# Loads of the first attention group in 112 + 16 rows, two more products of ones, and a new order of the opening pieces

## The chip, the cores and the metric

The kernel runs on one core of a Trainium2 chip. The metric is the device time of one execution in microseconds (us), lower is better. The profile is one further execution, taken by the hardware profiler. Its span runs from the first to the last instruction. TensorE (PE) does matrix products, VectorE (DVE) and ScalarE (ACT) work on elements, GpSimd (POOL) does a little set-up and issues some transfers, and SyncE (SP) only issues transfers.

## The reference

A normalised linear attention feeds a two-layer block with a gate. B = 8 batches, 8 heads, S = 576 positions, head width 64; the block has 4608 tokens, width 512 and hidden width 2048. All arrays come in as float64 or float32 and are multiplied in float32 or in two float32r parts.

```python
kv  = einsum('bhsd,bhse->bhde', k, v)
out = einsum('bhsd,bhde->bhse', q, kv)
x   = out / sqrt(mean(out*out, -1) + 1e-6) * g_norm     # then heads side by side: (B*S, 512)
h   = x @ w_in                                          # 512 -> 2048
g   = h * erf(softplus(h))
y   = g @ w_out                                         # 2048 -> 512
```

## The kernel before

**Groups.** The 4608 rows are taken as nine groups of 512: T = 0 to 7 are the first 512 positions of each batch, and T = 8 is made of the last 64 positions of all batches. A group needs its attention output transposed, `xT` (four slices, one for each pair of heads p = 0 to 3), before its first layer can start. The first two groups (T = 0 and 1, `FIRST = 2`) multiply plain float32; the later ones use weights cut into three float32r parts, written to DRAM and loaded back by SyncE.

**The opening, T = 0.** `load_pair` (L137) loads k, v and q of a pair of heads. `first_group(p)` (L712) defines thirteen small steps for a pair: `kv` (L717, products of k and v on TensorE), `kv_out` (L731, VectorE copies them to SBUF), `q` (L736, TensorE transposes q), `q_out` (L742, ScalarE copies), `result` (L746, TensorE), `square` (L749, ScalarE), `mean` (L752, TensorE), `log`, `root`, `again` (L756 to L763, ScalarE) and `norm_a`, `norm_b`, `norm_c` (L766 to L776, VectorE; the last writes slice p of `xT`). `tail`, `tail_out`, `tail_result` and `tail_kept` (L793 to L817) do the last 64 positions of batch 0. In what order all these steps are put into the programs of the engines is written out by hand in the string `ORDER`. No scheduler changes it: each engine takes its own instructions in the order in which the Python code issues them.

**The weights.** They come as float64 and are turned into float32 in 18 items (`w_order`, L301): w_in columns 0 to 3 one by one, then pairs of w_in or w_out tiles. An item is loaded (`load_w`, four raw buffers), split (`w_split`, L266) and joined (`w_join`, L277). `w_next(what)` (L308) takes the next item of that kind, with a counter of its own for load, split and join. A split of the opening gives ScalarE two instructions, e (L273) and m (L274). After the opening, `w_late` is set (L849) and a split gives it m alone; then the join begins with e on VectorE (L284). A join is L287, L290 and L297 on VectorE, and L297 reads e and m:

```python
    def weights():
        w_next("split")
        w_next("join")
        w_next("load")
```

`ORDER` holds five `split`, four `join` (each with a load) and four `fetch` (four of the waiting transfers of later batches each).

**The loop.** `for n in range(FIRST * FC + 1)` takes one 128-wide slice of the hidden layer at a time: products with w_in (L970), the copy out of PSUM (L983) and softplus (L1001) on ScalarE, erf after every fourth n (L915), the gate product `gates(n - 4)` on VectorE (L911), and `project(n - 5)` on TensorE (L673), which reads the gated slice and w_out. At n = 0 ten blocks are issued at once, of n = 0 to 2: `(0,0) (1,0) (0,1) (1,1) (2,0) (2,1) (0,2) (1,2) (2,2) (0,3)`, where (n, c) needs item n of w_in and slice c of `xT`; then come (1,3) at n = 1, (2,3) at n = 2, and four blocks for each n from 3 on. Whether `weights()` runs at an n, once before and once after the attention pieces of that n, is decided by `due` (L904) from the count of joins alone: items 4 to 9 are joined at n = 2, 4, 5, 6, 7, 8, items 10 and 11 at n = 9, 12 at 10, 13 at 11, items 14 and 15 at n = 12, 16 at 13 and 17 at 14. After the `weights()` of an n come the pieces of the next group's attention (`norm` and `turn`, then later `visit` with L432 to L446 on TensorE), and `gates` behind them.

**The start.** Two products of a 128x512 tile of ones (L828) run on TensorE while the first loads are under way.

Of the kernel before, what the change touches and what calls it, by code (L numbers as in the profile page):

```python
# [39 lines left out]
FP32 = mybir.dt.float32  # L40
# [17 lines left out]
SHIFT = 4096.0  # L58
SQ = 32
ORDER = """  # L60
kv0 q0 q_out0 kv_out0 result0 kv1 q1 square0 mean0 kv_out1 q_out1 log0 result1
kv2 kv_out2 root0 square1 q2 again0 q_out2 mean1 norm_a0 tail norm_b0 log1 tail_out
kv3 q3 root1 again1 q_out3 split norm_c0 kv_out3 tail_result result2 result3 square2 split mean2
next0 fetch square3 norm_a1 split mean3 log2 root2 norm_b1 tail_kept again2
join fetch log3 root3 join next1 again3 softplus norm_c1 join fetch norm_a2 split norm_b2 norm_c2 norm_a3
norm_b3 norm_c3 split join fetch
"""


# [1 line left out]
def kernel(  # L71
# [10 lines left out]
    nc = tc.nc  # L82
    P = 128
    B, H, S, D = q.shape
    DM, DF = moe_w_in.shape[0], moe_w_in.shape[1] // 2
    J = 4
    G = J * P
    R = S - G
    NP = H // 2
# [35 lines left out]

    q_last = early.tile([P, 2, 2, D], FP32, name="q_last", bufs=1)

    def chunks(T):

        return 6 if T == 0 else 5  # L130

    def rows_in(T, c):

        rows = S // chunks(T) // 16 * 16
        return rows + (S - chunks(T) * rows if c == 0 else 0)

    def load_pair(i, later=False):  # L137
        T, p = divmod(i, NP)
        if T >= B:
            return  # L140
        pool = early if i in (2, 3) else kvp
        for name, got, src in (("k", k_sb, k), ("v", v_sb, v)):
            side = nc.scalar if (i, name) == (0, "v") else nc.sync
            C = chunks(T)
            rows, rest = rows_in(T, 1), rows_in(T, 0) - rows_in(T, 1)
            t = got[T, p] = pool.tile([rows + rest, 2, C, D], FP32, name=f"{name}_sb", tag=name)
            heads = src[T, 2 * p : 2 * p + 2]
            due_ = [
                partial(
                    side.dma_start,  # L150
                    out=t[:rows].rearrange("r h c d -> r h (c d)"),
                    in_=heads[:, : S - rest].rearrange("h (r c) d -> r h (c d)", c=C),
                )
            ]
            if rest:
                due_.append(
                    partial(
                        side.dma_start,
                        out=t[rows:, :, 0],
                        in_=heads[:, S - rest :].rearrange("h r d -> r h d"),  # L160
                    )
                )
            if later:
                to_fetch.extend(due_)
            else:
                for start in due_:
                    start()
        if T > 0:
            load_q(i)
            return  # L170
        t = pool.tile([P, G if pool is early else S], FP32, name="q_sb", tag="q")
        t = q_sb[T, p] = t[:, 0:G].rearrange("p (j h d) -> p j h d", j=J, h=2)
        nc.sync.dma_start(
            out=t, in_=q[T, 2 * p : 2 * p + 2, 0:G, :].rearrange("h (p j) d -> p j h d", j=J)
        )
# [35 lines left out]
    ones = early.tile([P, G], I32, name="ones", tag="w_m", bufs=2).bitcast(FP32)  # L211
# [10 lines left out]
    bd_first = early.tile([P, 2, P], FP32, name="bd_first", bufs=1)  # L222
    nc.vector.memset(bd_first, 0.0)
    nc.gpsimd.memset(bd_kv, 0.0)
    for p in range(NP):
        nc.gpsimd.dma_start(
            out=q_last[p % 2 * R : p % 2 * R + R, p // 2],
            in_=q[0, 2 * p : 2 * p + 2, G:S, :].rearrange("h r d -> r h d"),
        )
    for i in range(2):  # L230
        nc.gpsimd.dma_start(
            out=g_col[i * D : i * D + D, :], in_=g_norm.rearrange("(d one) -> d one", one=1)
        )
# [120 lines left out]
    def kv_products(T, p, at, crossed):  # L354


        ks, vs = (x.pop((T, p)) for x in (k_sb, v_sb))
        C = chunks(T)
        for c in range(C):
            for r in range(2):  # L360
                rows = (slice(0, D), slice(D, rows_in(T, c)))[r]
                for i in range(2):
                    yield partial(
                        nc.tensor.matmul,
                        at[rows_of[i], 1 - (r ^ i) if crossed else r, kv_cols],
                        lhsT=ks[rows, i, c],
                        rhs=vs[rows, i, c],
                        start=(c == 0),
                        stop=(c == C - 1),
                    )  # L370

    def kv_kept(T, p, at):
# [339 lines left out]
    def first_group(p):  # L712

        st = {}
        bd = bd_first[:, p] if p < 2 else kv_of(0, p)

        def kv():  # L717
            st["kv"] = ps_at.tile([P, G], FP32, name="kv_ps", tag="at")
            ks, vs = (x.pop((0, p)) for x in (k_sb, v_sb))
            C = chunks(0)  # L720
            for c in range(C):
                for i, s in enumerate(rows_of):
                    nc.tensor.matmul(  # L723
                        st["kv"][s, s],
                        lhsT=ks[0 : S // C, i, c],
                        rhs=vs[0 : S // C, i, c],
                        start=(c == 0),
                        stop=(c == C - 1),
                    )

        def kv_out():  # L731
            kv_ps = st.pop("kv")
            for s in rows_of:
                nc.vector.tensor_copy(out=bd[s, s], in_=kv_ps[s, s])

        def q():  # L736
            o = st["o"] = ps_o.tile([P, G], FP32, name="o_ps", tag=f"o{p}")
            qs = q_sb.pop((0, p))
            for j in range(J):
                nc.tensor.transpose(o[:, j * P : j * P + P], qs[:, j], ident)  # L740

        def q_out():  # L742
            st["u"] = gate.tile([P, G], FP32, name="qT", tag="h")
            nc.scalar.copy(st["u"], st["o"])

        def result():  # L746
            nc.tensor.matmul(st["o"], lhsT=bd, rhs=st["u"], start=True, stop=True)  # L747

        def square():  # L749
            nc.scalar.activation(st["u"], st["o"], AF.Square)  # L750

        def mean():  # L752
            ms = st["ms"] = ps_h.tile([P, G], FP32, name="ms_ps", tag="h")
            nc.tensor.matmul(ms, lhsT=mean_w.bitcast(FP32), rhs=st["u"], start=True, stop=True)  # L754

        def log():  # L756
            st["r"] = gate.tile([P, G], FP32, name="rms_r", tag="s")
            nc.scalar.activation(st["r"], st["ms"], AF.Ln, bias=eps_col)

        def root():  # L760
            nc.scalar.activation(st["r"], st["r"], AF.Exp, scale=-0.5)

        def again():  # L763
            nc.scalar.activation(st["u"], st["r"], AF.Square)

        def norm_a():  # L766
            nc.vector.scalar_tensor_tensor(
                out=st["u"], in0=st.pop("ms"), scalar=EPS, in1=st["u"], op0=ALU.add, op1=ALU.mult
            )

        def norm_b():
            nc.vector.scalar_tensor_tensor(
                out=st["u"], in0=st["u"], scalar=3.0, in1=st.pop("r"), op0=ALU.subtract, op1=ALU.mult
            )

        def norm_c():  # L776
            if p == 0:
                xT[0] = wide.tile([P, KC, G], FP32, name="xT", tag="a")
            nc.vector.scalar_tensor_tensor(
                out=xT[0][:, p, :],  # L780
                in0=st.pop("o"),
                scalar=gm_col,
                in1=st.pop("u"),
                op0=ALU.mult,
                op1=ALU.mult,
            )

        steps = (kv, kv_out, q, q_out, result, square, mean, log, root, again, norm_a, norm_b, norm_c)
        return {step.__name__ + str(p): step for step in steps}

# [31 lines left out]
    def join_load():  # L822
        w_next("join")
        w_next("load")

    warm = ps_h.tile([P, G], FP32, name="warm_ps", tag="h")
    for _ in range(2):
        nc.tensor.matmul(warm, lhsT=ones[:, 0:P], rhs=ones, start=True, stop=True)  # L828
    for _ in range(RAW):
        w_next("load")  # L830
    do = {
# [1 line left out]
        "tail_out": tail_out,  # L833
        "tail_result": tail_result,
        "tail_kept": tail_kept,
        "split": partial(w_next, "split"),
        "softplus": softplus_table,
        "join": join_load,
# [78 lines left out]
    for n in range(FIRST * FC + 1):  # L917
        T, f = divmod(n, FC)
# [38 lines left out]
        elif T < FIRST:  # L957
# [11 lines left out]
            for i, c in blocks:  # L969
                nc.tensor.matmul(  # L970
                    plain[i],
                    lhsT=w_in_sb[:, i % FC, c],
                    rhs=xT[T][:, c, :],
                    start=(c == 0),
                    stop=(c == KC - 1),
                )
        if T < FIRST:
            if n == whole:
                old_h = acc.tile([P, BATCH, G], FP32, name="h", tag="e")
            h = hs[n] = old_h[:, n - whole] if n >= whole else unit("h_sb")  # L980
# [92 lines left out]
    for m in range(first_batch, batches + 1):  # L1073
        T, b = divmod(m, NB)
        todo = []
        last_ = b == NB - 1 and T + 1 < NG
        if T + 1 < NG:
            todo = list(attention(T + 1, b, in_parts=last_))
            if b == 0:
                side = late_r if T % 2 == FIRST % 2 else late  # L1080
# [135 lines left out]
```

## Time and profile before

| what | us |
|---|---|
| median of three timed runs | 907.28 (906.86 to 907.31) |
| the profiled execution's own time | 908.57 |
| its span | 906.8 |
| TensorE busy | 897.8 |
| VectorE busy | 749.3 |
| ScalarE busy | 593.4 |
| GpSimd busy | 4.7 |
| TensorE busy in 0 to 24 us | 20.52 |
| TensorE busy in 24 to 142 us | 117.75 |
| TensorE busy in 142 to 880 us | 737.14 |
| TensorE busy in 880 to 907 us | 22.38 |

A line of the timeline gives the start in us, the duration in us, the engine, the line of the code, the instruction, what it writes and reads, the tile's size and the number of instructions merged, and in square brackets how long the engine had been idle and what ended that. A line of windows gives for each stretch its length, then the busy time of PE, PE's weight loads, DVE, ACT and POOL with the number of instructions, then the granted TensorE clock as a share of full speed, the busy share of the DMA engines and GB/s. A float32 product shows as two MATMUL records.

### The profile page before, as it was taken

How to read it: one execution, taken by the hardware profiler on the slowest of the kernel's cores; microseconds unless marked ns; L12 is line 12 of the kernel's file. 1: busy time of each engine (PE TensorE's matmuls, PEld its weight loads, DVE VectorE, ACT ScalarE, POOL GpSimd, SP SyncE). 2: the span in 40 equal slices, each digit the busy share in tenths (PEclk: the TensorE clock that was granted, in tenths of full speed). 3: DMA queues.
4: the chain of work that ended last, by engine and by line, in shares of the span. 5: the costliest groups of instructions: out<-in, count | busy, mean ns of one | idle time of the engine just before them, and what ended most of it. 6: DMA issues, size and time to landing. Idle time of an engine off the chain costs nothing.

```text
span 906.8 us, 13592 instructions
## 1 busy us (share of the span) xinstructions
PE 897.8 (99%) x4994; PEld 667.9 (74%) x4994; DVE 749.3 (83%) x1085; ACT 593.4 (65%) x784; POOL 4.7 (1%) x14
## 2 busy tenths in 40 slices
PE   8999999999999999999999999999999999999998
PEld 4444446666678888888888888888888888888886
DVE  4899958997688888888888888888888888887777
ACT  5976667775766666666666666666666666665552
POOL 2000000000000000000000000000000000000000
PEclk9999999999999999999999999999999999999999
DMA  9978408999699999999899989999897788778871
GB/s 275 296 213 238 113 16 292 357 357 348 204 342 338 331 325 297 354 324 311 282 315 340 319 280 313 349 328 307 270 352 271 266 315 306 288 282 323 313 265 49
DMA packets 145506, 259.91 MB, mean 287 GB/s; under 512 B 81504, under 2 KB 104032, under 8 KB 145440
## 3 DMA queue, kind: packets, MB, share of 16 engines
q1 hardware_dynamic: 144640, 258.09, 84.7%
q10 hardware_dynamic: 608, 0.82, 0.3%
q8 instruction: 40, 0.66, 0.3%
q14 instruction: 26, 0.21, 0.1%
q0 software_dynamic: 192, 0.13, 0.1%
HBM read 224.40 MB, written 34.60 MB: 286 GB/s over the span
## 4 chain that ended last, share of the span: by engine, by line
PE 94%; ACT 2%; DMA 2%; DVE 1%; issue 0%; SPq 0%; DVEq 0%; ACTq 0%
PE n_ps L617 48%; PE m_ps L617 24%; PE o_ps L673 10%; PE h_ps L970 6%; PE at_ps L446 2%; PE at_ps L432 2%; DMA w_out_parts<-w_out 1%; PE at_ps L484 1%; PE at_ps L485 1%; DMA q_sb<-in_q_dram 1%; PE ms_ps L754 0%; PE o_ps L747 0%; PE kv_ps L723 0%; PE o_ps L740 0%; DVE h L911 0%
## 5 line engine op out<-in xcount | busy, mean ns | idle before, releaser
L617 PE MATMUL n_ps<-w_out_parts,g_forms 128*128 128x512 f32 x928 | 230.5, 390 | 0.6 <-DMA w_out_parts<-w_out 0.6
L617 PE MATMUL n_ps<-x_forms,w_in_parts 128*128 128x512 f32 x896 | 224.3, 392 | 0.0
L617 PEld LDWEIGHTS n_ps<-w_out_parts,g_forms 128*128 128x128 f32 x928 | 172.7, 188 | 36.5 <-DMA w_out_parts<-w_out 1.1
L617 PEld LDWEIGHTS n_ps<-x_forms,w_in_parts 128*128 128x128 f32 x896 | 166.6, 188 | 35.7 <-issue 0.2
L595 DVE TENSOR_TENSOR h<-m_ps,h 128x512 f32<-128x512 f32 x116 | 78.1, 687 | 69.0 <-PE m_ps L617 67.5
L617 PE MATMUL m_ps<-w_out_parts,g_forms 128*128 128x512 f32 (+1 forms) x468 | 124.2, 388 | 0.0
L617 PE MATMUL m_ps<-x_forms,w_in_parts 128*128 128x512 f32 x448 | 119.7, 389 | 0.0
L1122 ACT ACTIVATE h<-n_ps 128x512 f32<-128x512 f32 x112 | 66.2, 594 | 74.7 <-PE n_ps L617 74.5
L1127 ACT ACTIVATE s<-h 128x512 f32<-128x512 f32 x112 | 68.3, 629 | 69.7 <-DVE h L595 69.7
L673 PE MATMUL o_ps<-w_out_sb,h_sb 128*128 128x512 f32 x224 | 101.5, 596 | 0.2 <-DVE h_sb L911 0.2
L617 PEld LDWEIGHTS m_ps<-w_out_parts,g_forms 128*128 128x128 f32 x468 | 87.4, 188 | 18.4
L617 PEld LDWEIGHTS m_ps<-x_forms,w_in_parts 128*128 128x128 f32 x448 | 84.1, 188 | 17.5
L595 DVE TENSOR_TENSOR e<-m_ps,e 128x512 f32<-128x512 f32 (+1 forms) x117 | 80.3, 687 | 15.8 <-PE m_ps L617 5.6
L673 PEld LDWEIGHTS o_ps<-w_out_sb,h_sb 128*128 128x128 f32 x224 | 41.3, 189 | 45.2 <-issue 43.1
L561 DVE SCALAR_TENSOR_TENSOR g_forms<-g_forms 128x1024 fp32r<-128x1024 f32 x58 | 71.1, 1225 | 2.0
L558 DVE TENSOR_TENSOR g_forms<-h,g_forms 128x1024 fp32r<-128x1024 f32 x58 | 70.5, 1216 | 1.2 <-ACT g_forms L555 1.1
L555 ACT ACTIVATE g_forms<-h 128x1024 fp32r<-128x1024 f32 x58 | 58.4, 1048 | 15.2 <-PE m_ps L617 11.1
L590 DVE SCALAR_TENSOR_TENSOR e<-n_ps,e 128x512 f32<-128x512 f32 x88 | 60.2, 684 | 7.9 <-PE n_ps L617 7.9
L1176 DVE TENSOR_TENSOR h<-h,s 128x1024 f32<-128x1024 f32 x56 | 65.9, 1218 | 0.0
L970 PE MATMUL h_ps<-xT,w_in_sb 128*128 128x512 f32 x144 | 65.0, 596 | 0.2 <-DVE w_in_sb L297 0.2
L118 ACT ACT_TABLE_LOAD x44 | 56.5, 1283 | 0.8
L970 PEld LDWEIGHTS h_ps<-xT,w_in_sb 128*128 128x128 f32 x144 | 26.9, 190 | 34.5 <-issue 30.1
(133 smaller groups left out, 992.8 us busy)
## 6 DMA issues: line engine op xcount, KB each, us to landing
w_out_parts<-w_out SPq DMA_DIRECT2D x116, 768.0 KB, 7.4
w_in_parts<-w_in SPq DMA_DIRECT2D x112, 768.0 KB, 7.0
w_in<-w_new SPq DMA_DIRECT2D x16, 768.0 KB, 4.8
w_raw<-in_moe_w_in_dram SPq DMA_DIRECT2D x16, 512.0 KB, 5.7
w_raw<-in_moe_w_out_dram SPq DMA_DIRECT2D x8, 1024.0 KB, 5.8
out_dram<-e SPq DMA_DIRECT2D x32, 256.0 KB, 3.6
k_sb<-in_k_dram SPq DMA_DIRECT2D x28, 280.0 KB, 7.5
v_sb<-in_v_dram SPq DMA_DIRECT2D x28, 280.0 KB, 7.5
```

Of the source, the lines that this page charges most:

```text
L118: nc.scalar.preload_act_table_set("softplus")
L555: nc.scalar.activation(high, x, AF.Copy, scale=1.0 + 2.0**-13)
L558: nc.vector.tensor_tensor(out=low, in0=x, in1=high.bitcast(FP32), op=ALU.subtract)
L561: nc.vector.scalar_tensor_tensor(out=both, in0=low.bitcast(FP32), scalar=SHIFT, in1=high.bitcast(FP32), op0=ALU.mult, op1=ALU.add,)
L590: nc.vector.scalar_tensor_tensor(out=out_, in0=ps, scalar=scale, in1=out_, op0=ALU.mult, op1=ALU.add)
L595: nc.vector.tensor_tensor(out=out_, in0=ps, in1=out_, op=ALU.add)
L617: nc.tensor.matmul(ps[:, cols], lhsT=weights(form, k), rhs=moving(form, k)[:, cols], start=(form == forms[0] and k == 0), stop=(form == fo ...
L673: nc.tensor.matmul(o_ps[j], lhsT=g[:, j * P : j * P + P], rhs=w_out_sb[:, f, :], start=(f == 0), stop=last,)
L970: nc.tensor.matmul(plain[i], lhsT=w_in_sb[:, i % FC, c], rhs=xT[T][:, c, :], start=(c == 0), stop=(c == KC - 1),)
L1122: nc.scalar.activation(h[:, i], n_ps, AF.Copy, scale=SHIFT - 1.0)
L1127: nc.scalar.activation(s[:, i], h[:, i], AF.Softplus)
L1176: nc.vector.tensor_tensor(out=part(h, half), in0=part(h, half), in1=part(s, half), op=ALU.mult)
```

## The change

k and v of T = 0 were held as 96 rows of six chunks of 64 numbers a head; they become 112 rows of five chunks, with the last 16 positions as rows 112 to 127 of chunk 0, as the later groups have them already. So a k or v of T = 0 takes two transfers. The second, of 16 rows, is issued on the same queue for pair 0, and by GpSimd for pairs 1 to 3: four ahead of GpSimd's loads of `q_last` and two behind them, ahead of those of `g_col`. The products of k and v are five a head and not six. Two more products of ones are named `fill0` (256 columns) and `fill1` (384 columns) and stand in the order behind `kv0` and `q0`. `ORDER` is rewritten; it now holds four `split`, four `join` and five `fetch`.

```diff
 ORDER = """
-kv0 q0 q_out0 kv_out0 result0 kv1 q1 square0 mean0 kv_out1 q_out1 log0 result1
-kv2 kv_out2 root0 square1 q2 again0 q_out2 mean1 norm_a0 tail norm_b0 log1 tail_out
-kv3 q3 root1 again1 q_out3 split norm_c0 kv_out3 tail_result result2 result3 square2 split mean2
-next0 fetch square3 norm_a1 split mean3 log2 root2 norm_b1 tail_kept again2
-join fetch log3 root3 join next1 again3 softplus norm_c1 join fetch norm_a2 split norm_b2 norm_c2 norm_a3
-norm_b3 norm_c3 split join fetch
+kv0 fill0 q0 fill1 kv_out0 q_out0 result0 square0 kv1 q1 q_out1 mean0 log0 kv_out1 result1 root0
+kv2 tail square1 mean1 kv_out2 again0 q2 tail_out norm_a0 kv3 q3 norm_b0 norm_c0 log1 root1 kv_out3
+again1 q_out2 q_out3 norm_a1 split tail_result result3 norm_b1 norm_c1 result2 tail_kept square3
+next0 fetch join split square2 fetch join next1 split mean3 mean2 log2 root2 fetch again2 join fetch log3 root3
+norm_a2 again3 norm_b2 split norm_c2 norm_a3 norm_b3 softplus join norm_c3 fetch
 """
...
-    def chunks(T):
-
-        return 6 if T == 0 else 5
-
-    def rows_in(T, c):
-
-        rows = S // chunks(T) // 16 * 16
-        return rows + (S - chunks(T) * rows if c == 0 else 0)
+    CH = 5
+    ROWS = S // CH // 16 * 16
+    REST = S - CH * ROWS
+
+    rests = []
 
     def load_pair(i, later=False):
         T, p = divmod(i, NP)
@@ -140,26 +136,27 @@
             return
         pool = early if i in (2, 3) else kvp
         for name, got, src in (("k", k_sb, k), ("v", v_sb, v)):
-            side = nc.scalar if (i, name) == (0, "v") else nc.sync
-            C = chunks(T)
-            rows, rest = rows_in(T, 1), rows_in(T, 0) - rows_in(T, 1)
-            t = got[T, p] = pool.tile([rows + rest, 2, C, D], FP32, name=f"{name}_sb", tag=name)
+            side, side_r = (nc.scalar if (i, name) == (0, "v") else nc.sync,) * 2
+            if 0 < i < NP:
+                side_r = nc.gpsimd
+            t = got[T, p] = pool.tile([ROWS + REST, 2, CH, D], FP32, name=f"{name}_sb", tag=name)
             heads = src[T, 2 * p : 2 * p + 2]
             due_ = [
                 partial(
                     side.dma_start,
-                    out=t[:rows].rearrange("r h c d -> r h (c d)"),
-                    in_=heads[:, : S - rest].rearrange("h (r c) d -> r h (c d)", c=C),
+                    out=t[:ROWS].rearrange("r h c d -> r h (c d)"),
+                    in_=heads[:, : S - REST].rearrange("h (r c) d -> r h (c d)", c=CH),
                 )
             ]
-            if rest:
-                due_.append(
-                    partial(
-                        side.dma_start,
-                        out=t[rows:, :, 0],
-                        in_=heads[:, S - rest :].rearrange("h r d -> r h d"),
-                    )
+            due_.append(
+                partial(
+                    side_r.dma_start,
+                    out=t[ROWS:, :, 0],
+                    in_=heads[:, S - REST :].rearrange("h r d -> r h d"),
                 )
+            )
+            if 0 < i < NP:
+                rests.append(due_.pop())
...
     nc.gpsimd.memset(bd_kv, 0.0)
+    for start in rests[:4]:
+        start()
     for p in range(NP):
         nc.gpsimd.dma_start(
             out=q_last[p % 2 * R : p % 2 * R + R, p // 2],
             in_=q[0, 2 * p : 2 * p + 2, G:S, :].rearrange("h r d -> r h d"),
         )
+    for start in rests[4:]:
+        start()
...
             st["kv"] = ps_at.tile([P, G], FP32, name="kv_ps", tag="at")
             ks, vs = (x.pop((0, p)) for x in (k_sb, v_sb))
-            C = chunks(0)
-            for c in range(C):
+            for c in range(CH):
+                rows = slice(0, ROWS if c else ROWS + REST)
                 for i, s in enumerate(rows_of):
                     nc.tensor.matmul(
                         st["kv"][s, s],
-                        lhsT=ks[0 : S // C, i, c],
-                        rhs=vs[0 : S // C, i, c],
+                        lhsT=ks[rows, i, c],
+                        rhs=vs[rows, i, c],
                         start=(c == 0),
-                        stop=(c == C - 1),
+                        stop=(c == CH - 1),
                     )
 
...
+    def fill(n):
+        nc.tensor.matmul(warm[:, 0:n], lhsT=ones[:, 0:P], rhs=ones[:, 0:n], start=True, stop=True)
+
     warm = ps_h.tile([P, G], FP32, name="warm_ps", tag="h")
     for _ in range(2):
-        nc.tensor.matmul(warm, lhsT=ones[:, 0:P], rhs=ones, start=True, stop=True)
+        fill(G)
...
+        "fill0": partial(fill, 2 * P),
+        "fill1": partial(fill, 3 * P),
```

In `kv_products` the same constants `CH`, `ROWS` and `REST` take the place of `chunks` and `rows_in`; there the sizes are those it had.

More of the change, by code (lines that the diff above doesn't have):

```diff
@@ L357, in kv_products @@
         ks, vs = (x.pop((T, p)) for x in (k_sb, v_sb))
-        C = chunks(T)
-        for c in range(C):
+        for c in range(CH):
             for r in range(2):
-                rows = (slice(0, D), slice(D, rows_in(T, c)))[r]
+                rows = (slice(0, D), slice(D, ROWS if c else ROWS + REST))[r]
                 for i in range(2):
@@ L719, in kv @@
             ks, vs = (x.pop((0, p)) for x in (k_sb, v_sb))
-            C = chunks(0)
-            for c in range(C):
+            for c in range(CH):
+                rows = slice(0, ROWS if c else ROWS + REST)
                 for i, s in enumerate(rows_of):
@@ L724, in kv @@
                         st["kv"][s, s],
-                        lhsT=ks[0 : S // C, i, c],
-                        rhs=vs[0 : S // C, i, c],
+                        lhsT=ks[rows, i, c],
+                        rhs=vs[rows, i, c],
                         start=(c == 0),
-                        stop=(c == C - 1),
+                        stop=(c == CH - 1),
                     )
```

## The prediction

> **What bounds the kernel now.** I read the page first, then windows, then the timeline of each engine over the opening and over the loop. The page's busy line and its chain by engine:
>
> ```profile
> PE 897.8 (99%) x4994; PEld 667.9 (74%) x4994; DVE 749.3 (83%) x1085; ACT 593.4 (65%) x784; POOL 4.7 (1%) x14
> PE 94%; ACT 2%; DMA 2%; DVE 1%; issue 0%; SPq 0%; DVEq 0%; ACTq 0%
> ```
>
> TensorE is busy all the time and the chain is TensorE. So a microsecond counts only where TensorE stands still or runs slowly. The windows say where that is:
>
> ```profile
> 5.00:8.00 3.00, 1.77 (x29) 1.23 (x28) 0.44 (x2) 0.31 (x1) 0.10 (x1) 1.00 1.12 274
> 8.00:9.00 1.00, 0.67 (x1) 0.34 (x2) 0.00 (x0) 0.28 (x1) 0.00 (x0) 0.77 1.23 294
> 9.00:11.00 2.00, 2.00 (x18) 0.83 (x18) 0.00 (x0) 0.60 (x1) 0.22 (x1) 0.50 1.11 257
> 11.00:12.00 1.00, 1.00 (x16) 0.88 (x14) 0.22 (x1) 0.00 (x0) 0.00 (x0) 0.53 1.21 288
> ...
> 24.00:60.00 36.00, 35.75 (x171) 16.34 (x171) 30.03 (x45) 31.11 (x42) 0.00 (x0) 1.00 0.96 289
> 60.00:142.00 82.00, 82.00 (x396) 38.56 (x395) 67.46 (x96) 54.77 (x72) 0.00 (x0) 1.00 0.47 136
> ```
>
> The reader is to see two things. TensorE's clock is halved from about 8.4 to 11.9 us, after 5 to 8 us in which it was busy only 1.77 of 3. And from 24 us on it has nothing to spare: any stall put into the loop is paid whole. The opening's timeline:
>
> ```profile
> 8.33 1.91 PE L747 MATMUL o_ps<-qT,bd_first 128*128 128x512 f32 x2 [0.67 <-ACT qT L744]
> 10.18 1.55 PE L723 MATMUL kv_ps<-v_sb,k_sb 96*64 96x64 f32 x24
> 14.16 0.92 PE L723 MATMUL kv_ps<-v_sb,k_sb 96*64 96x64 f32 x24
> 23.29 14.43 PE L970 MATMUL h_ps<-xT,w_in_sb 128*128 128x512 f32 x32
> 15.20 0.46 DVE L734 COPY bd_kv<-kv_ps 64x64 f32<-64x64 f32 x2 [2.97 <-PE kv_ps L723]
> 30.17 0.75 DVE L779 SCALAR_TENSOR_TENSOR xT<-o_ps,gm_col,qT 128x512 f32<-128x512 f32 x1
> ```
>
> The same products take 1.55 us at half clock and 0.92 at full. VectorE works without a gap from `kv_out2` (15.20) to the last slice of `xT` (30.92). And the loop at n = 12, ScalarE, VectorE and TensorE:
>
> ```profile
> 101.13 1.28 ACT L118 ACT_TABLE_LOAD   x1
> 102.42 2.22 ACT L274 ACTIVATE w_m<-w_raw 128x1024 int32<-128x1024 uint32 x2
> 96.30 1.23 DVE L297 CUSTOM_DVE_ANT_0 w_in_sb<-w_e,w_m 128x2048 uint16<-128x2048 uint16 x1
> 103.62 1.23 DVE L297 CUSTOM_DVE_ANT_0 w_out_sb<-w_e,w_m 128x2048 uint16<-128x2048 uint16 x1 [0.40 <-ACT w_m L274]
> 104.76 0.68 DVE L911 TENSOR_TENSOR h_sb<-h_sb,s_sb 128x512 f32<-128x512 f32 x1
> 108.42 3.70 PE L673 MATMUL o_ps<-w_out_sb,h_sb 128*128 128x512 f32 x8
> ```
>
> The join at 96.30 is item 14; its m had been made at n = 11, since splits run one item ahead of joins. The two m at 102.42 are items 15 and 16. Item 15 is joined at once and even waits 0.40 us for its m.
>
> **What the Trainium skill says.** "TensorE: Matmul & The Clock Gate", Part 1, says that the clock is halved after an idle window of about 3.4 us and restored after a busy one, and that the windows run free. The trace agrees in size (half clock from about 8.4 to 11.9 us) but shows a halving after a window only partly idle. The same page, "Architectural detail", says that ScalarE and VectorE take their queues strictly in order; the 0.40 us wait, with L911 behind it, agrees. "DMA: Bandwidth & Descriptors", "Issuing engines are not separate DMA queues", says that transfers issued by different engines share the same DMA engines; the windows agree (257 to 294 GB/s, DMA engines full, from 5 us on), so GpSimd saves SyncE's time to issue, not bandwidth.
>
> **The change part by part.**
>
> *Products of k and v.* Ten products of a pair for twelve: 0.92 to about 0.77 us, four times, 0.6 us less TensorE. All lie ahead of waits for loads or for VectorE, so it is worth something only through kv1 below.
>
> *Fills.* A 512-column record takes 0.43 us at full clock (eight in 3.43) and 0.95 cold. fill0 is half of two records, 0.43 us; fill1 three quarters, 0.64. They lie in the waits of 0.48 us (for q, landing 1.18 + 5.71 = 6.89) and 0.67 us (for ScalarE's copy), so at full clock they cost nothing. They lift the busy share of the window before 8.5 from 1.9 of 3.4 us to 2.9. No window of the trace lies between, so whether that holds the clock is unknown: bounds 0 and the full loss. I take it that it holds: result0 1.91 to about 0.95, kv1 1.55 to 0.77.
>
> *Transfers.* Bytes are the same. k and v of pair 1 land at 2.69 + 6.5 = 9.2 and q of pair 1 at 3.75 + 6.5 = 10.25, so kv1 goes from 10.18 to 9.25 and q1 from 11.66 to 10.3, no earlier. Pair 0's extra piece takes SyncE some 0.4 us ahead of q of pair 0 (a small one took 0.46), hidden only if the DMA engines stay full. Bounds: 0.4 us sooner (128 rows might load better than 96) and 0.45 later; I take 0. On GpSimd six issues of 0.61 to 0.79 us come ahead of `g_col`: issued at 7.8 and not 4.0, landing after 5.9, at about 14.5 with the second, so `gm_col` is there by 15.0; norm_c0 needs it at 15.8. The cover is 0.8 us, after which it would be paid one to one. `q_last` is late by 2.5 us: about 11.5, needed at 13.4.
>
> *Order of the opening.* I set each engine's instructions end to end, each starting when its engine and its inputs are free, by these rows. result1 ends at 12.64, kv2 at 13.36, kv_out2 starts at 13.46, 1.7 us sooner. From there VectorE has two kv_out (1.0), two tail copies (0.7), four norms (8.4) and, new, four joins of 1.9 and not three ahead of norm_c3 (7.6): 17.7 us, end 31.2, against 15.20 + 15.8 = 31.0 before (traced 30.92). The fourth join has been put ahead of norm_c3. TensorE starts L970 at 21.9 instead of 23.29, waits some 0.5 us for the join of item 1, runs its nine blocks, and stands 1.1 us at block (0,3) for norm_c3. Seven more blocks of 0.86 end at 37.3; before, 37.65. Of 1.4 us gained **0.4 stays**. SyncE's moved `next0`, `next1` and `fetch` issue the same 24 transfers; pair 4's k is needed at 37.65 and landed at 24.05, so nothing.
>
> *One split fewer.* ScalarE loses the early split of item 4 (2.3 us at 30.0 to 32.2, where it would have waited 0.42 for TensorE anyway). But now every `weights()` splits the item it joins: **L297 waits for the m issued beside it**, and in VectorE's queue behind it lie norm, turn, halve and the gate product, for which TensorE waits. I go through the slots of L274.
> - n = 2: m done about 35.7, L297 to 37.0, needed 38.0: nothing.
> - n = 4: L297 from 42.87 to 45.0, gate product done at 46.85, just when L673 needs it; item 6 then 51.6 against 51.46: **0.1**.
> - n = 5 to 8: up to 1.4 us of VectorE, under 2 us or more of cover.
> - n = 9: m done at 77.5, L297 from 73.30 to 77.55. Behind it 8.0 us of norm, turn and the join of item 11, then the gate product: done 86.25, needed 85.86: **0.4**.
> - n = 12: m of item 14 stands behind Ln, Exp, two table loads and erf and is done at 103.55. L297 from 96.30 to 103.6. Behind it by spacings 1.14, norm 0.72, 0.73, 0.79, turn 0.70, join of item 15 0.69, 0.72, 1.36, 1.14, gate product 0.68: 112.27. L673 wants it at 108.42: **3.9**, between 3.3 and 4.5 by how tightly those spacings close.
> - n = 13 and 14: 1 us of cover or more is left.
>
> TensorE has no later wait that could give this back (the windows from 60 us).
>
> Sum: -0.4 + 0.1 + 0.4 + 3.9 = +4.0 us. Span 906.8 to 910.8; the profiled execution 908.57 to 912.6; its median stands 1.3 below that: 907.28 + 4.0 = **911.3**.
>
> **The rivals.**
> 1. *The clock is halved all the same.* Speaking for it: the halving before came after a window with half its time busy. Then kv_out2 gains nothing much and the fourth join still stands ahead: block (0,3) about 1.2 later. 911.3 + 1.2 = 912.5.
> 2. *Not slower: the wait for m at n = 12 is covered.* TensorE needs the gated slice at 108.42 and had it at 105.44. If m of item 14 is done by 99.7 (96.3 plus 3.0 plus the 0.4 wait that goes), nothing is late; from there each us costs one. Speaking for it: ScalarE is only 65% busy. Against: its queue is in order, and Ln to erf fill 94.3 to 102.4. It would give 907.28 - 0.4 + 0.1 = 907.0, and with all of the opening's 1.4 us and faster loads kept some 905.4.
> 3. *The new transfers come late* (GpSimd's pieces, `g_col`, SyncE's extra issue): VectorE's chain to norm_c3 moves by up to 0.9: 912.2.
>
> **How the numbers follow.** Forecast 0.60, first rival 0.18, second 0.14 (of it 0.03 below 905.47), third 0.08. The range takes the forecast with its bounds (3.3 to 4.5, loads 0.4 either way), the first and the third: 909 to 913.4. 0.2% is 1.8 us, about what a measurement of this kernel can tell from no change. Faster 0.03, same 0.12, slower 0.85.
>
> **What would show it.** Right: L297 of w_in at n = 12 with some 3.6 us idle ended by ACT w_m L274, and L673 right after it idle about 3.9 on DVE h_sb L911; full clock from 8 to 12; L970 starting near 22 with about 1 us idle on DVE xT near 30; norm_c3 ending near 31.2. Wrong: no PE wait over 1 us between 60 and 142, or a first L970 block at 22 that carries its lead to n = 4.

## The result and the profile after

| | before | after |
|---|---|---|
| median, us | 907.29 (906.86 to 909.71, 4 runs) | 915.03 (914.33 to 916.24, 4 runs) |
| profiled execution's own time | 908.57 | 914.91 |
| its span | 906.8 | 913.1 |
| TensorE busy | 897.8 | 899.4 |

The changed kernel is slower: the ratio is 1.0081, interval 1.0061 to 1.0102. That is 7.7 us in the medians and 6.3 us in the spans. The forecast was 4.0. In the changed kernel's listing L911 is L916, L970 is L975, L297 is L298 and L274 is L275.

The page's busy line and the chain of work that ended last, by engine, after:

```profile
PE 899.4 (98%) x4982; PEld 668.0 (73%) x4982; DVE 750.2 (82%) x1086; ACT 591.9 (65%) x783; POOL 7.7 (1%) x20
PE 87%; DVE 4%; DMA 3%; ACT 2%; issue 1%; SPq 1%; DVEq 0%; ACTq 0%
```

TensorE's share of the chain fell from 94% to 87%, and VectorE's rose from 1% to 4%: TensorE now waits for VectorE. TensorE is also busy 1.6 us longer, although its products are much the same (12 records fewer; the two fills add about as many columns as the shorter products of k and v save). The table of waits of TensorE (what waited, for whom, us in total, times, longest) says where:

```profile
PE o_ps L673 <- DVE h_sb L916: 3.6, 3, 3.1
PE at_ps L432 <- ACT h_sb L988: 0.7, 1, 0.7
PE h_ps L975 <- DVE xT L779: 0.7, 1, 0.7
PE h_ps L975 <- DVE w_in_sb L298: 0.6, 2, 0.3
```

The first line is the gate product for `project`. The second is put down to ScalarE's copy, which came last. But the visit (L432) also reads the transposed q, which VectorE finished at 108.58, and before, the visit did not need that copy, since it started ahead of it (TensorE and ScalarE, before):

```profile
107.13 0.66 PE L432 MATMUL at_ps<-qT,bd_kv 64*64 64x256 f32 x8
107.23 0.59 ACT L983 COPY h_sb<-h_ps 128x512 f32<-128x512 f32 x1 [0.38 <-PE h_ps L970]
```

So both waits hang on VectorE's queue. The timeline around n = 12, ScalarE, VectorE and TensorE, after:

```profile
101.95 1.28 ACT L117 ACT_TABLE_LOAD   x1
103.24 2.18 ACT L275 ACTIVATE w_m<-w_raw 128x1024 int32<-128x1024 uint32 x2
...
104.43 1.23 DVE L298 CUSTOM_DVE_ANT_0 w_in_sb<-w_e,w_m 128x2048 uint16<-128x2048 uint16 x1 [4.14 <-ACT w_m L275]
107.80 0.78 DVE L353 STREAM_TRANSPOSE qT<-q_sb 128x576 f32<-128x576 f32 x1
111.28 1.23 DVE L298 CUSTOM_DVE_ANT_0 w_out_sb<-w_e,w_m 128x2048 uint16<-128x2048 uint16 x1
112.43 0.69 DVE L916 TENSOR_TENSOR h_sb<-h_sb,s_sb 128x512 f32<-128x512 f32 x1
...
108.73 0.66 PE L432 MATMUL at_ps<-qT,bd_kv 64*64 64x256 f32 x8 [0.69 <-ACT h_sb L988]
113.17 5.40 PE L673 MATMUL o_ps<-w_out_sb,h_sb 128*128 128x512 f32 x8 [3.08 <-DVE h_sb L916]
```

The join of item 14 stands 4.14 us until its m, made only after the table load at 101.95. Norm, turn and the join of item 15 follow it without a gap, and the gate product comes at 112.43. TensorE stands 0.69 and 3.08 us. Then the same eight products take 5.40 us; before they took 3.70. Windows after (length, busy PE, PEld, DVE, ACT, POOL, then the clock):

```profile
112.00:114.00 2.00, 0.83 (x2) 0.49 (x3) 1.97 (x4) 1.16 (x1) 0.00 (x0) 1.00 0.36 58
114.00:117.00 3.00, 3.00 (x5) 1.28 (x4) 2.83 (x4) 0.00 (x0) 0.00 (x0) 0.51 0.00 0
117.00:118.00 1.00, 1.00 (x3) 0.28 (x3) 1.00 (x3) 0.00 (x0) 0.00 (x0) 0.75 0.00 0
```

The clock is halved from about 114.1 to 117.5 us, after TensorE has stood still and is working again. The opening after, TensorE and the last slice of `xT` on VectorE:

```profile
8.36 1.12 PE L747 MATMUL o_ps<-qT,bd_first 128*128 128x512 f32 x2
9.61 0.80 PE L723 MATMUL kv_ps<-v_sb,k_sb 128*64 128x64 f32 x20
22.55 1.02 PE L975 MATMUL h_ps<-xT,w_in_sb 128*128 128x512 f32 x2
23.90 7.11 PE L975 MATMUL h_ps<-xT,w_in_sb 128*128 128x512 f32 x16 [0.33 <-DVE w_in_sb L298]
31.69 6.28 PE L975 MATMUL h_ps<-xT,w_in_sb 128*128 128x512 f32 x14 [0.68 <-DVE xT L779]
37.90 0.81 PE L391 MATMUL at_ps<-v_sb,k_sb 64*64 64x64 f32 x40
...
30.89 0.75 DVE L779 SCALAR_TENSOR_TENSOR xT<-o_ps,gm_col,qT 128x512 f32<-128x512 f32 x1
```

The clock stays full here: result0 takes 1.12 and not 1.91 us. The loop starts at 22.55 and not 23.29, waits 0.33 us for a join and 0.68 us for the last slice, and reaches the products of k and v of T = 1 (L391) at 37.90. Before, it was there at 37.65:

```profile
37.65 0.81 PE L391 MATMUL at_ps<-v_sb,k_sb 64*64 64x64 f32 x40
```

### The profile page after: what moved, and what is told of

The parts are those of the page before. It is cut to its first block, busy times and chain, and to the rows that moved or that the text cites. A ratio compares the mean times of both kernels' runs of the same rounds, so it can differ in the third digit from the quotient of the medians.

```text
span 913.1 us, 13585 instructions
## 1 busy us (share of the span) xinstructions
PE 899.4 (98%) x4982; PEld 668.0 (73%) x4982; DVE 750.2 (82%) x1086; ACT 591.9 (65%) x783; POOL 7.7 (1%) x20
## 4 chain that ended last, share of the span: by engine, by line
PE 87%; DVE 4%; DMA 3%; ACT 2%; issue 1%; SPq 1%; DVEq 0%; ACTq 0%
PE n_ps L617 47%; PE m_ps L617 24%; PE o_ps L673 8%; PE h_ps L975 4%; PE at_ps L446 2%; PE at_ps L432 2%; DMA w_out_parts<-w_out 1%; DMA k_sb<-in_k_dram 1%; DVE w_e L291 1%; DMA v_sb<-in_v_dram 1%; SPq L164 1%; PE at_ps L484 1%; PE at_ps L485 1%; DVE w_in_sb L298 1%; ACT L117 0%
## 5 line engine op out<-in xcount | busy, mean ns | idle before, releaser
L975 PE MATMUL h_ps<-xT,w_in_sb 128*128 128x512 f32 x144 | 65.1, 596 | 1.3 <-DVE xT L779 0.7
L975 PEld LDWEIGHTS h_ps<-xT,w_in_sb 128*128 128x128 f32 x144 | 26.9, 190 | 35.5 <-issue 32.2
```

What stands on the lines that cost most here:

```text
L975: nc.tensor.matmul(plain[i], lhsT=w_in_sb[:, i % FC, c], rhs=xT[T][:, c, :], start=(c == 0), stop=(c == KC - 1),)
```

## The experiments

The theory after the result: the missing split makes VectorE wait for ScalarE, TensorE therefore stands (has nothing to do) at n = 10 and n = 13, and the last stand halves the clock. The rivals: the loss comes from the opening (loads, order), or the slow `project` has another cause. All ratios are to the kernel before, run beside on the same chip; its medians there were 907.98 (39 runs, experiments 1 to 4), 907.90 (49, experiments 5 to 8, on another chip) and 907.73 (43, experiments 9 to 12).

**1. The fifth split put back.**

```diff
-norm_a2 again3 norm_b2 split norm_c2 norm_a3 norm_b3 softplus join norm_c3 fetch
+norm_a2 again3 norm_b2 split norm_c2 norm_a3 norm_b3 softplus join norm_c3 split fetch
```

> The changed kernel with a fifth split at the end of the opening's order, nothing else. Theory (the missing split makes VectorE wait for ScalarE at n = 9 and n = 12, TensorE then stands 0.3, 0.7 and 3.1 us, and the last stand halves TensorE's clock for 1.8 us more): all of these go, about 5.9 us of the 6.3 us that the span grew by; span near 907.2 where the changed kernel had 913.1, median near 909. Rival (the loss comes from the opening, from later loads and the order, and the waits in the loop would only move): span stays above 911.5, with a wait of over 2 us between 60 and 142 us or a later start of the loop.

Measured: 908.94 us median, ratio 1.0007 (1.0000 to 1.0015), span 907.7. TensorE's waits in this trace from the first block's products on, without the reloads of weights:

```profile
PE h_ps L975 <- DVE xT L779: 0.7, 1, 0.7
PE h_ps L975 <- DVE w_in_sb L298: 0.4, 2, 0.2
PE o_ps L673 <- DVE h_sb L916: 0.2, 1, 0.2
```

Between 60 and 130 us no wait is left. The median falls by 6.1 us (915.03 to 908.94), so one word of the order carries most of the loss. What remains is up to 1.4 us above the kernel before by the interval.

**2. The kernel before without its fifth split.**

```diff
-norm_b3 norm_c3 split join fetch
+norm_b3 norm_c3 join fetch
```

> The kernel before with its fifth split taken out of the order, nothing else: loads, products and the order of all else as before. Theory (missing split): span and median grow by 5 to 6.5 us, with L297 at n = 12 waiting about 4 us for m and project(8) then 3 to 4 us, and half clock behind it. Rival (the loss needs the new loads or the new order): within 1 us of the kernel before.

Measured: 914.33 us, ratio 1.0083 (1.0057 to 1.0109), span 912.0. VectorE's join of item 14 and TensorE's `project` at n = 13:

```profile
102.50 1.23 DVE L297 CUSTOM_DVE_ANT_0 w_in_sb<-w_e,w_m 128x2048 uint16<-128x2048 uint16 x1 [4.09 <-ACT w_m L274]
111.25 6.11 PE L673 MATMUL o_ps<-w_out_sb,h_sb 128*128 128x512 f32 x8 [3.08 <-DVE h_sb L911]
```

The old loads and the old order show the same stand and an even slower `project`. This execution also ran at full speed in its opening from result0 on, without fills:

```profile
8.20 1.12 PE L747 MATMUL o_ps<-qT,bd_first 128*128 128x512 f32 x2 [0.68 <-ACT qT L744]
21.93 14.13 PE L970 MATMUL h_ps<-xT,w_in_sb 128*128 128x512 f32 x32
35.99 0.81 PE L391 MATMUL at_ps<-v_sb,k_sb 64*64 64x64 f32 x40
```

The old opening at full clock is at 35.99 where the profiled execution of before, at half clock, was at 37.65. So half the clock in the opening belongs to single executions and not to the kernel.

**3. The fifth split at n = 11.**

```diff
         while due(0):
             weights()
+        if n == 11:
+            w_next("split")
```

> The changed kernel with the fifth split not in the opening but at n = 11, ahead of the erf, so that only the joins from n = 12 on find their m made. If n = 12 is the place, as the theory says, 0.7 + 3.1 + 1.8 = 5.6 us come back, and the 0.3 us at n = 9 stay: span near 907.5. If the waits at n = 4 and n = 9 carry a loss that shows up only at n = 12 (a backlog of VectorE), less than half of it comes back: span above 910.

Measured: 909.03 us, ratio 1.0010 (1.0004 to 1.0017), span 907.4. The waits of VectorE at n = 2 to 9 are all still there (3.06 us for item 10), TensorE's wait at n = 10 is 0.33 us, and at n = 13 there is none. VectorE's join of item 10 and TensorE's `project` at n = 10:

```profile
77.67 1.23 DVE L298 CUSTOM_DVE_ANT_0 w_in_sb<-w_e,w_m 128x2048 uint16<-128x2048 uint16 x1 [3.06 <-ACT w_m L275]
86.40 3.70 PE L673 MATMUL o_ps<-w_out_sb,h_sb 128*128 128x512 f32 x8 [0.33 <-DVE h_sb L916]
```

So of the 5.7 us by which the span fell, all but 0.3 (this opening reached L391 at 37.60 and not 37.90) hang on the joins from n = 12 on; the waits ahead of them leave VectorE no work in arrears.

**4. Products in the stand ahead of `project` at n = 13.**

```diff
...
+            if n == 13:
+                for i in range(13):
+                    nc.tensor.matmul(
+                        at_now[0][:, i % 2, 3 * P : 4 * P],
+                        lhsT=mean_w.bitcast(FP32),
+                        rhs=mean_w.bitcast(FP32),
+                        start=True,
+                        stop=True,
+                    )
             project(f2, hs[n - LAG], last)
```

`at_now` holds the PSUM tile that the visit just ahead has taken, and `mean_w` is a constant.

> The changed kernel with thirteen small products of a constant (128 columns, some 0.2 us each, 2.8 us together) put into TensorE's wait ahead of project(8) at n = 13; their values are overwritten and used by nobody. If the halved clock after the 3.1 us stand is a cost of its own, project(8) runs in 3.6 us and not 5.4, and the span falls by 1.7 us to about 911.4, while the wait for the gate product ends at the same place. If the slow project has another cause (its operands, memory), nothing changes: 913.1, or up to 0.3 more for the extra products.

Measured: 914.13 us, ratio 1.0070 (1.0052 to 1.0087), span 911.6. TensorE at n = 13:

```profile
108.75 0.66 PE L434 MATMUL at_ps<-qT,bd_kv 64*64 64x256 f32 x8 [0.68 <-ACT h_sb L990]
110.84 3.17 PE L1023 MATMUL at_ps<-mean_w 128*128 128x128 f32 x26 [0.73 <-ACT qT L453]
113.84 3.60 PE L675 MATMUL o_ps<-w_out_sb,h_sb 128*128 128x512 f32 x8
```

`project` takes 3.60 us again. The products themselves had to wait 0.73 us for ScalarE's reading of the tile and so ended 0.7 us too late, which the expectation had not foreseen. So 1.8 us were gained and 0.7 lost at n = 13; the span fell by 1.5, so some 0.4 of that lies elsewhere. The intervals of this kernel and of the changed one overlap (medians 914.13 and 915.03), so the times alone don't show it. The clock does: all four runs of the changed kernel have a mean clock (the granted clock averaged over the run) of 0.998 or less, and all four here are above that. The halved clock is a cost of its own, and the slow `project` doesn't come from its operands.

**5. The kernel before with the fills alone.**

```diff
-kv0 q0 q_out0 kv_out0 result0 kv1 q1 square0 mean0 kv_out1 q_out1 log0 result1
+kv0 fill0 q0 fill1 q_out0 kv_out0 result0 kv1 q1 square0 mean0 kv_out1 q_out1 log0 result1
...
```

`fill0` and `fill1` are defined as in the change.

> The kernel before with the two extra products of ones alone; loads, order and splits as before. Theory (the opening of the kernel before has half clock only in some executions, by where the clock's window falls; in the execution of the second experiment it had full clock without them, and its loop reached the products of k and v of T = 1 at 35.99 us, not 37.65): the fills keep full clock, so the spread of the runs shrinks and the median falls by 0.5 to 1.3 us. Rival (the fills only lengthen the opening, since TensorE had the wait for nothing): median 0 to 1 us higher.

Measured: 907.45 us, ratio 0.9991 (0.9981 to 1.0001), span 905.1. The median is 0.45 us lower, a little short of what was expected, and the interval just touches no difference. Taken together, the runs say more. Seven kernels with fills and without the stand at n = 13 were run 107 times, and none had a mean clock at or below 0.998. Of 131 runs of the kernel before, 21 had; their median was 908.8 to 909.1 in the three groups, that of the others 907.5 to 907.8. The recorded clock misses some slow openings (experiment 6), so the times count too: 32 of the 131 took 909.5 us or more, 24 of them with a mean clock above 0.998. Of the 40 runs of the old order with fills (experiments 5, 10 and 11) none did; the highest is 909.27.

**6. The kernel before with the new loads alone.** The edit is the change without its new `ORDER` (and so without the fills).

> The kernel before with the 112 + 16 rows and GpSimd's pieces alone; its own order with five splits, no fills. Theory: the loads land 0.3 to 0.5 us later (k and v of pair 3: 15.0 and 15.95 us against 14.5 and 15.4), the products of k and v are 0.12 us shorter each; median 0 to 0.5 us higher. Rival (the new loads are what makes the opening of the changed kernel late): median over 1 us higher.

Measured: 909.02 us, ratio 1.0010 (1.0002 to 1.0018): 1.1 us in the medians, more than the theory allowed and just past the rival's bound of 1 us, though the interval reaches from 0.2 to 1.6. In its profiled execution q of pair 0 came later, and TensorE's products ran at half speed from the first ones of k and v on (TensorE, then a window):

```profile
5.22 1.33 PE L724 MATMUL kv_ps<-v_sb,k_sb 128*64 128x64 f32 x20
7.25 1.08 PE L741 MATMUL o_ps<-ident,q_sb 128*128 128x128 f32 x4 [0.70 <-DMA q_sb<-in_q_dram]
9.01 2.08 PE L748 MATMUL o_ps<-qT,bd_first 128*128 128x512 f32 x2 [0.68 <-ACT qT L745]
9.00:10.00 1.00, 0.99 (x1) 0.50 (x2) 0.00 (x0) 0.00 (x0) 0.00 (x0) 1.00 1.10 291
```

result0 takes 2.08 us where it takes 1.12 at full speed, yet the clock column reads 1.00. So in this trace the record misses a clock that has not yet risen, and a count by mean clock can be too low. By that count 13 of the 21 runs had 0.998 or less; the kernel before had 8 of 49 beside it.

**7. The changed kernel with the fifth split, and norm_c3 ahead of the fourth join.**

```diff
-norm_a2 again3 norm_b2 split norm_c2 norm_a3 norm_b3 softplus join norm_c3 fetch
+norm_a2 again3 norm_b2 split norm_c2 norm_a3 norm_b3 softplus norm_c3 join split fetch
```

> The changed kernel with the fifth split and with norm_c3 put ahead of the fourth join; nothing else. In the changed kernel TensorE stands 0.68 us at block (0,3) for the last slice of xT. Theory (the fourth join ahead of it is why): that wait goes and 0.7 us come back against the first experiment, median near 908.2. Rival (VectorE is late as a whole, so that the next block waits for the join instead): within 0.2 us of the first experiment.

Measured: 908.00 us, ratio 1.0001 (0.9993 to 1.0010), span 906.2. The wait of 0.68 us for `xT` is gone. The median is 0.9 us below experiment 1, though the two ran on different chips and their intervals overlap; the trace, not the time, shows what the place of norm_c3 does.

**8. The changed kernel with the fifth split, without the fills.**

```diff
-kv0 fill0 q0 fill1 kv_out0 q_out0 result0 square0 kv1 q1 q_out1 mean0 log0 kv_out1 result1 root0
+kv0 q0 kv_out0 q_out0 result0 square0 kv1 q1 q_out1 mean0 log0 kv_out1 result1 root0
...
-norm_a2 again3 norm_b2 split norm_c2 norm_a3 norm_b3 softplus join norm_c3 fetch
+norm_a2 again3 norm_b2 split norm_c2 norm_a3 norm_b3 softplus join norm_c3 split fetch
```

> The changed kernel with the fifth split and without the two fills; new loads and new order kept. Theory (the fills keep the clock full in the opening): the runs spread over 2 to 3 us as those of the kernel before do, where those of the first experiment lie within 1.6 us, and the median lies 0.3 to 1 us above the first experiment's 908.94. Rival (fills do nothing for the clock): same median and spread as the first experiment, or up to 0.3 us lower.

Measured: 910.31 us (908.10 to 911.72), ratio 1.0023 (1.0012 to 1.0033), against 1.0007 (1.0000 to 1.0015) with the fills. The fills are worth about 1.4 us here by the medians, more than the 0.3 to 1 expected, though the two ran on different chips and the intervals just overlap. The runs spread over 3.6 us, those with the fills over 1.6. Its opening, TensorE:

```profile
7.31 0.63 PE L740 MATMUL o_ps<-ident,q_sb 128*128 128x128 f32 x4 [1.31 <-DMA q_sb<-in_q_dram]
8.61 2.08 PE L747 MATMUL o_ps<-qT,bd_first 128*128 128x512 f32 x2 [0.68 <-ACT qT L744]
10.62 1.34 PE L723 MATMUL kv_ps<-v_sb,k_sb 128*64 128x64 f32 x20
```

TensorE waits 1.31 and 0.68 us where the fills stood, and result0 runs at half clock.

**9. New loads alone, pair 0's k piece by GpSimd.** Experiment 6 with this edit; the first condition changes in a second place too, and the second bound with it.

```diff
-            if 0 < i < NP:
+            if i < NP and (i, name) != (0, "v"):
                 side_r = nc.gpsimd
...
-    for start in rests[:4]:
+    for start in rests[:5]:
         start()
```

> The kernel before with the new loads alone, as in the sixth experiment, but the 16 rows of k of pair 0 issued by GpSimd ahead of its other pieces and not by SyncE ahead of q of pair 0 (v of pair 0 stays on ScalarE). Theory (SyncE's extra issue of 0.45 us leaves the DMA engines short of work: all runs with the new loads move only about 200 GB/s from 4 to 5 us, those with the old ones 260 to 277): the dip goes, q of pair 0 is transposed by 7.05 us and not 7.25 or later, and the median falls by 0.5 us or more from 909.02. Rival (the many small pieces as such are slow): the dip stays, median within 0.3 of 909.02.

Measured: 908.30 us, ratio 1.0004 (0.9996 to 1.0013). From 4 to 5 us 280 GB/s were moved (206 in experiment 6) and q of pair 0 was transposed from 6.97. Its trace and its median (0.7 us lower, on another chip; 0.5 by the ratios) are on the side of the theory; the intervals of 6 and 9 overlap, so the time alone doesn't show it. Nor is the dip as even as the expectation has it: the traces with the piece on SyncE moved 184 to 246 GB/s from 4 to 5 us.

**10. Fills and new loads, pair 0's k piece by GpSimd.** Experiment 9 with the fills of experiment 5.

> The kernel before with the fills and with the new loads, pair 0's k piece by GpSimd; its own order with five splits. If the loads then cost nothing, their shorter products (0.12 us for each pair) are all that is left of them: median 907.0 to 907.5, where the fills alone gave 907.45. If small pieces cost bandwidth wherever they are issued: 907.8 or more.

Measured: 907.56 us, ratio 0.9992 (0.9981 to 1.0004), between its two expectations and nearer the first. In this trace the products of pair 0 waited 1.10 us for k, so moving the piece shifts a delay as well.

**11. Fills and new loads as in the change.** Experiment 6 with the fills of experiment 5.

> The kernel before with the fills and with the new loads exactly as in the changed kernel; its own order with five splits. Theory (the new loads as issued cost some 0.5 to 1 us by pair 0's extra piece on SyncE): median 907.9 to 908.5, above the next lower experiment with that piece on GpSimd by 0.5 or more. Rival (the loads cost only while the clock is half): within 0.2 of 907.45.

Measured: 907.52 us, ratio 0.9998 (0.9990 to 1.0006). The theory missed and its rival held: with the fills the new loads cost nothing that can be told, wherever pair 0's piece is issued. So what they cost in experiment 6 seems to go through the clock: a later q lengthens TensorE's wait, and more executions run at half clock behind it. The counts of experiment 6 and its trace fit this; no run separates it from other ways in which the fills could hide the loads.

**12. Everything mended in the new order.** Experiment 7 with pair 0's piece as in experiment 9.

> The changed kernel with the fifth split, norm_c3 ahead of the fourth join, and pair 0's k piece by GpSimd: everything found so far mended, the rest of the new order kept. Theory (loads, splits and the place of norm_c3 are all that is wrong with it): 907.3 to 907.6, as good as the kernel before with fills, 0.5 below the seventh experiment's 908.0. Rival (the rest of the new order costs too): 908.0 or more, above the kernel with the old order and the same loads by over 0.5.

Measured: 907.88 us, ratio 0.9997 (0.9988 to 1.0006). It lies between the two expectations, 0.3 us above experiments 10 and 11 with the old order. So the rest of the new order costs little, if anything, and brings nothing. Nor does any of these kernels beat the kernel before beyond its interval; the fills alone come nearest.

## Why the prediction was half right

| step, us | forecast | profiles |
|---|---|---|
| opening, to the products of k and v of T = 1 | -0.4 | +0.25 (37.65 to 37.90) |
| wait at n = 6 | +0.1 | +0.06 (0.21 to 0.27) |
| n = 9, wait at n = 10 | +0.4 | +0.33 |
| n = 12, waits at n = 13 | +3.9 | +3.77 (0.69 + 3.08) |
| clock behind them | none | +1.7 (3.70 to 5.40) |
| all else | 0 | +0.2 |
| span | +4.0 | +6.3 (906.8 to 913.1) |

**One split fewer: right, in place and size.** Slots of L274, the queue behind L297 and the gate product came as written, but TensorE's 3.77 us of waiting fell into two parts, since the visit waits for the transposed q in the same queue (0.69), which the prediction had not seen; the m of item 14 was done 4.14 us after VectorE was ready for it, and experiments 1 to 3 show by undoing, by doing alone and by moving that this word of the order is the cause.

**The step that failed: 3.9 us as the whole price of the wait at n = 12.** The prediction had quoted both halves of what was needed: that the clock falls after a wait, and that TensorE would stand 3.9 us. It applied the first only to the opening. Experiment 4 shows the missing term: with TensorE kept at work in that stand, `project` takes 3.60 us and not 5.40. The halved clock adds 1.7 us to the 3.8 us of waiting in the changed kernel's profile, and 2.4 in that of experiment 2.

**The opening: a gain that wasn't there.** The other terms that failed are the opening's 0.4 us and the base of the sum. The walk along the queues held in part: the lead of the first block was 0.74 us where 1.4 was forecast, with loads landing some 0.3 to 0.6 us later (v of pair 3 let its products start at 16.09), which had been left as a bound; norm_c3 ended at 31.64 for 31.2, and the fourth join ahead of it was paid, as experiment 7 shows.

**The base of the sum.** The opening was compared with a profiled execution whose clock had been halved there. Its own time stood 1.3 us above the median, which the prediction noted and did not ask about. Experiment 2 shows the old opening 1.66 us faster in an execution at full clock, and 99 of the 131 runs of the kernel before took less than 909.5 us, so the fills give most of them little, while the later last slice and the joins are paid by all. This fits 6.3 us between the two profiles and 7.7 between the medians; it is argued from single traces and from times, not shown run by run. After the split is put back, 1.0 us is left (experiment 1), which is gone in experiments 7 and 12.

**The rivals.** The first (the clock halved in the opening all the same) did not come true: result0 took 1.12 or 1.13 us in all nine traces with the fills, and 1.91 or 2.08 in three of the five without them. The second (wait covered) is refuted; its sum had also left out the 0.4 us of n = 9. The third, late loads, was part of the truth: loads landed some 0.3 to 0.6 us late and norm_c3 ended 0.4 us late, within its bound of 0.9.

## What to carry to other kernels

When two counters hand work from one engine to another (split here, join there), what matters is how many steps one runs ahead of the other: here a lead of nought turned the longest stretch of ScalarE's queue (logarithm, exponential, erf and their table loads) into 4.1 us of waiting for VectorE. Price a stand of the matrix engine with what follows it: here one of 3.08 us cost another 1.7 to 2.4 us, because the work behind it ran at half clock. And before a stretch of a profile is taken as what a change can win, ask whether the timed runs have it too; an execution that is above its own median is a warning. A clock column of 1.00 is not enough: compare the duration of a product whose size is known.

## What the runs showed of the hardware

In the changed kernel the granted clock fell to half at about 114.1 us, 0.9 us after TensorE had resumed work at 113.17, and was full again at about 117.5 (0.51 in 114 to 117 is 0.06 us at full clock, 0.75 in 117 to 118 is half of it): 3.4 us. In experiment 2 it had fallen before `project` began, at about 109.3, and was back at about 116.1 (0.65 in 109 to 110, 0.93 in 116 to 117): 6.8 us, so `project` ran 6.11 us there. The same stand of 3.08 us thus cost 1.7 and 2.4 us. The Trainium skill, "TensorE: Matmul & The Clock Gate", Part 1, says that the clock is set by windows of about 3.4 us that run free; stretches of once and twice that length agree. It puts the fall down to an idle window, and here the measurement differs: in the 3.4 us ahead of the two falls TensorE had been busy 0.9 and 1.6 us, and 1.85 us ahead of the fall in the opening of before.

Two products of 256 and 384 columns, in waits of 0.5 to 1.3 us, were followed by a result0 at full speed in nine traces of nine. GpSimd took 0.51 to 0.73 us for each of its six small issues, where 0.61 to 0.79 had been priced. With SyncE's one extra issue of 0.45 us, q of pair 0 was issued 0.5 us later (1.68 and not 1.18), and its products started at 7.06 to 8.25 us in the traces with that issue, at 7.03 before. Why that differs so much between executions stays open.
